# A new hand-written order of work for a two-layer attention kernel, with its loads on one queue

## The chip, the cores and the metric

The kernel runs on one core of a Trainium2 chip. The metric is the time of the whole kernel on the device in microseconds (us), the median of several runs. The profile is of one execution; its span, from the first to the last instruction, is not quite the same number.

## What is computed

Two layers in a row. The first is attention with a local window and a few global keys; the second is a mixture of four attention experts, of which two are taken for each token.

```python
# layer 1: B=4, H=8, S=768, D=64; n_global=8, n_local=96
scores = q @ k.T / sqrt(D) - slope[h] * dist      # dist capped at n_local for global keys
keep   = (key < n_global) | (0 <= row - key < n_local)
x      = softmax(where(keep, scores, -1e9)) @ v   # heads joined: x is [4, 768, 512]
# layer 2: 4 experts of width 64
w      = softmax over the two largest of x @ w_gate
for e in range(4):
    ye   = softmax(causal((x @ wq[e]) @ (x @ wk[e]).T / 8)) @ (x @ wv[e]) @ wo[e]
    out += w[e] * ye                               # for the tokens that chose e
```

## The kernel before

**Tiles.** The work is cut into 24 units of 128 rows: unit u is row block u % 6 of batch u // 6. q, k and v come from memory in float32 and are cast to float16. Layer 1 of a unit: load and cast of q, k, v; transposes of k and q by TensorE (`turn`, L262 to L276) with a copy out of PSUM into kqT; local scores in two halves (`local_scores`, L321: bias by a matmul at L334, k times q at L341, exponential on ScalarE at L344); the few global keys for three units at a time (`global_scores`, L302); the product with v (`local_values`, L360, matmuls at L371) and the division by the row sums into x (L380); a transpose of x (`turn_x`, L383, copy at L390). Layer 2 of a unit: projections to k and q (`project_qk`, L392, matmuls at L401, copy at L406) and to v with the gate (`project_v`, L408, L415, copy at L417); the choice of two experts (`top_two`, L508, in steps); causal scores (L431, matmuls L446, exponential L449), the mask on GpSimd (L461), the product with v (L464, matmuls L474), a transpose (L488) and the output projection (L497, matmul L502, copy L505, store L506).

**Order.** There is no loop over units. The table ORDER, from L760 on, is a list of 658 short names, and a loop at L727 calls one function for each. The schedule is manual: every engine works its own instructions strictly in this order, and waits come from data and buffers. A name has a stage, a number and, where there is a choice, a letter for who does it:

```python
copies = {"a": S_.copy, "g": G.tensor_copy, "v": V.tensor_copy}
queues = {"s": dma, "a": S_.dma_start}
...
for slot in ORDER.split():
    stage, *args = stages[slot[:2]]
    if slot[-1].isalpha():
        args.append(slot[-1])
    stage(int(slot[2:].rstrip("agsv")), *args)
```

The letters on casts and copies are ScalarE (a), GpSimd (g), VectorE (v). On loads, s is the sync engine's queue (SP), which computes nothing, and a is ScalarE's, which must reach the issue in its own order. The names spoken of below: lk, lq load k or q of a unit (0.262 MB, L227). lv loads values (L245, L247): lv0 and lv1 are four pieces of 64 KB each, lv2 to lv5 two of 128 KB, all of batch 0; from lv6 on each is two pieces of 192 KB, and four of them, for four head pairs, make a batch. So a cast of a unit of batch 1 (vc6 to vc11) needs all of lv6 to lv9. wi0 to wi3 load the weights wk, wq, wv (with the gate) and wo (0.524 MB each); wc cast them. kc, qc, vc are casts; tk, tq transposes of k and q; sa, sb local scores; gi, gs, vg, vs the global keys; va, vb attention times v; tx the transpose of x; pk, pq, pv the projections; ro a step of the routing; ca, cb, cc causal scores; ma the mask; za, zb causal times v; tz, ou transpose and output.

**Buffers that make a load or a stage wait.** Four raw buffers each for q and k (a load waits for the cast four units back), two for v by batch, two for weights (wi2 waits for wc0); in PSUM two for scores (psS), one for the products with v (psZ), two for everything else (psT). Stores go on SP's queue too.

Of the kernel before, what the change touches and what calls it, by code (L numbers as in the profile page):

```python
# [757 lines left out]


ORDER = """  # L760
az0 lq0s xb0 lk0s qc0g kc0g tk0 lv0a lk1a vc0g lq1s lk2s kc1g lk3s lq2a lq3s lq4a xg0 tq0a lk4s
tk1 qc1g tq1v wi0a kc2a gi0 kc3v vs0 lv1s sa0 tk2 lq5s qc2g tq2v tk3 lk5a az1 az2 az3 sb0 qc3g
tq3v az4 gs0 vg0 qc4g kc4g lq6s tk4 lv2s wi1a tq4v lk6a sa1 sa2 va0 vb0 sb1 sa3 lv3s kc5v vc1g
lv4s lv5a vg1 va1 vb1 qc5g qc6g sb2 lk7s tk5 tq5v lq7s wc0g wi2a lk8a lk9s tx0v tx1v wc1g kc6v
sa4 sa5 pk0 pk1 lq8s pq0v vc2g vc3v vc4g pq1v vc5g sb3 vg2 gs1 tk6 kc7v lv6s va2 ca0 vb2 lq9a
tq6v sb4 sb5 lk10s lk11a qc7g wc2g tk7 tq7v vg3 va3 tx2v kc8g vb3 kc9v sa6 sb6 lv7s pv0v pv1a
vg4 va4 qc8g qc9g vb4 lv8a lv9s pk2 pq2a tk8 tq8v kc10v lk12s ca1 lk13a vg5 lq10s lq11s va5
tx3v lq12s tk9 tq9v gi1 gs2 tx4v vb5 pv2a pv3a sa7 sa8 tx5v ma0 pk3 ro0 vc6g ro0 vc7v vc8v pq3a
pv4v sb7 ro0 vs1 kc11v pk4 pq4a lq13s tk10 qc10v vc9g kc12v tq10v ca2 cb2 vg6 va6 ro0 vb6 tk11
qc11g ma1 tq11v pv5v ca3 vg7 va7 vb7 cb3 tk12 qc12g tq12v pk5 ro0 qc13g ro0 pq5a ro0 sb8 ro1  # L770
ro1 lv10s gs3 lk14s lk15s tx6v tx7v vg8 va8 vb8 lq14s lq15s lq16s ca4 pv6v pv7v kc13g lk16s
lk17s wi3a qc14v kc14g za0 zb0 sa9 sb9 pk6 pq6a tk13 ro1 tq13v cb4 cc4 ro1 lq17s lq18s qc15g
lv11s vg9 ro1 va9 lv12s tx8v tk14 tq14v vb9 kc15g kc16g lk18s ma2 ma3 ca5 pk7 pq7v tk15 tq15a
sa10 ro1 sb10 za1 pv8v vc10g vc11g qc16g ro1 zb1 pk8 pq8v kc17v tz0a sa11 sa12 vg10 va10 vb10
tz1a lv13s qc17g qc18g ro2 wc3g tk16 tq16v sb11 sb12 tk17 tq17v vg11 ca6 va11 lq19s vb11 gi2
gs4 ou0v ro2 tx9a sa13 sb13 kc18g ma4 vc12g za2 zb2 vc13g vc14g pk9 pq9a vc15g lk19s tx10v vs2
vc16g gs5 tz2v vc17a qc19g pv9v za3 ou1v ca7 cb5 ro2 tx11v lv14s zb3 ro2 pk10 pq10v ou2a vg12
va12 vb12 lk20s lq20s cc5 kc19g lq21a sa14 tk18 tq18v tk19 lk21s tq19v za4 zb4 ro2 ro2 pk11
lv15s pq11a tx12v ca8 vg13 ma5 va13 cb8 ro2 vb13 pv10v pv11a sa15 sa16 ma6 ro3 za5 ma7 tz3v
tx13v ro3 ro3 ro3 zb5 tz4a ro3 sb14 sb15 gi3 pk12 pq12a kc20g pv12v kc21g ca9 cb9 za6 zb6 pk13  # L780
lk22s pq13v kc22g tz5v ma8 ca10 lq22s vg14 va14 vb14 lv16s lv17s ma9 ou3a ou4v sa17 sa18 tz6v
za7 zb7 qc20g tk20 tq20v lk23s tx14v vc18g lq23s cb10 cc10 vg15 va15 vb15 ou5a ou6v sb16 vs3
tx15v ro3 za8 pv13v zb8 pv14a ca11 ca12 pk14 pq14v ro3 za9 vc19g tz7a zb9 sb17 sa19 tz8v ou7v
ma10 gs6 vg16 va16 vb16 qc21g cb11 cc11 ou8v tk21 qc22a tq21v za10 zb10 pk15 pq15a tx16v sb18
sb19 tz9v ro4 tz10v vg17 va17 vb17 ca13 ou9v ou10a vg18 qc23g va18 kc23v vc20g ca14 cb14 ro4
vb18 tk22 pk16 pq16a tq22v ma11 vg19 va19 vb19 ro4 ro4 ro4 ca15 cb15 pv15v pv16v za11 zb11
tx17a sa20 sa21 tx18v ro4 pk17 pq17v pv17a sb20 sb21 vc21g tk23 tq23v tz11a vc22g vg20 va20
vb20 ca16 gs7 ro4 tx19v ro5 pk18 pq18a pk19 ma12 za12 zb12 vc23g pq19a tx20v sa22 sa23 ro5
tz12v ma13 za13 zb13 pv18v ro5 ro5 ma14 ou11a ca17 ro5 vg21 va21 vb21 pk20 pq20v ro5 ro5 pv19a
sb22 sb23 tz13v za14 zb14 tx21v pv20a cb16 cc16 ro6 vg22 ro6 va22 vb22 ou12v ou13a ca18 vg23  # L790
va23 vb23 ro6 ma15 ma16 tx22v pv21a cb17 cc17 ro6 ro6 za15 tz14v zb15 ma17 pk21 pq21v ca19
tx23v za16 tz15v ma18 zb16 pv22a ro6 ro6 pv23a ro7 ca20 cb20 za17 tz16v zb17 ou14a pk22 pq22v
ro7 ro7 ca21 ma19 za18 zb18 ma20 ou15a ou16v ro7 ro7 ca22 cb21 za19 zb19 tz17v pk23 pq23v cb22
ma21 ro7 tz18v za20 zb20 ro7 cc22 ma22 ou17v ca23 tz19v cb23 za21 zb21 ou18v cc23 tz20v za22
zb22 tz21a ou19v ou20a ma23 za23 zb23 tz22a ou21a ou22a tz23v ou23a xt0
"""

MAXB = 512
# [38 lines left out]
```

## Time and profile before

The time is 159.45 us, the median of three runs (159.31 to 162.35). The span of the profiled execution is 160.6 us, TensorE's granted clock 0.946 on average.

| engine | busy us | share of the span | instructions |
|---|---|---|---|
| TensorE, matmul | 134.7 | 84% | 2950 |
| TensorE, weight load | 105.8 | 66% | 2950 |
| VectorE | 112.0 | 70% | 343 |
| ScalarE | 105.4 | 66% | 171 |
| GpSimd | 71.1 | 44% | 187 |

Read from memory are 20.98 MB, written 6.29 MB. SP's queue moved 21.63 MB, ScalarE's 5.65 MB. DMA-issuing instructions aren't counted as busy, so ScalarE's 66% doesn't hold the time in which it issues loads or waits to issue them; the rows named ACTq in a timeline do. Matmuls are pipelined, so a busy TensorE is not one at its peak. In sums by stretch the columns are: length, then busy us (and instructions) of PE, PEld, DVE, ACT and POOL, then the granted clock, the DMA share and GB/s.

### The profile page before, as it was taken

The numbers are of one execution on the slowest core, as the hardware profiler recorded it, in microseconds if no ns is written. First come the engines' busy times: TensorE is split into PE (matmuls) and PEld (weight loads), VectorE is DVE, ScalarE is ACT, GpSimd is POOL, SyncE is SP. The second block draws the span as 40 slices with busy tenths as digits, with TensorE's granted clock in tenths as the row PEclk, the third lists the DMA queues.
The fourth block names the chain that finished last, engine by engine and source line by source line (L and its number), as shares of the span: only waits on it lengthen the run. The fifth ranks groups of instructions, "written<-read, shape, count | busy, mean of one in ns | idle before, by whom it ended". The sixth has DMA issues, their size and how long they took to land.

```text
span 160.6 us, 6996 instructions
## 1 busy us (share of the span) xinstructions
PE 134.7 (84%) x2950; PEld 105.8 (66%) x2950; DVE 112.0 (70%) x343; ACT 105.4 (66%) x171; POOL 71.1 (44%) x187
## 2 busy tenths in 40 slices
PE   0266585779999999899999999999999999999710
PEld 0143363758778879787798876887889778776300
DVE  7978424248769977597796588788866788798530
ACT  0283051074648878788968988989878788799520
POOL 4454343093308463976636643603435254633100
PEclk9999558778999999999999999999999999999995
DMA  5999998999999989795499999032100103042550
GB/s 115 273 288 257 260 236 180 270 257 224 241 256 247 255 189 284 169 225 140 126 227 232 228 293 251 33 131 76 65 6 0 69 6 135 0 172 93 200 208 8
DMA packets 85623, 27.80 MB, mean 173 GB/s; under 512 B 82256, under 2 KB 82256, under 8 KB 85584
## 3 DMA queue, kind: packets, MB, share of 16 engines
q1 hardware_dynamic: 64480, 21.63, 53.6%
q10 hardware_dynamic: 21104, 5.65, 15.8%
q8 instruction: 25, 0.41, 1.1%
q14 instruction: 14, 0.11, 0.2%
HBM read 20.98 MB, written 6.29 MB: 170 GB/s over the span
## 4 chain that ended last, share of the span: by engine, by line
PE 60%; DMA 16%; ACTq 5%; SPq 4%; DVE 3%; ACT 2%; issue 2%; POOL 2%; POOLq 0%
DMA vf<-in_v_dram 11%; PE pps L401 11%; PE vps L415 7%; PE cps L446 6%; PE zps L371 6%; PE tp L267 6%; PE zps L474 5%; PE ops L502 4%; PE sps L334 4%; PE xps L386 4%; SPq L247 3%; DMA kf<-in_k_dram 3%; PE sps L341 3%; ACTq L157 3%; PE zps L356 2%; DMA out_dram<-osb 2%
## 5 line engine op out<-in xcount | busy, mean ns | idle before, releaser
L449 ACT ACTIVATE a<-cps 128x1024 f16<-128x1024 f32 (+1 forms) x48 | 42.0, 915 | 5.7 <-PE cps L446 5.1
L344 ACT ACTIVATE abuf<-sps 128x636 f16<-128x636 f32 (+1 forms) x48 | 30.7, 684 | 20.3 <-PE sps L341 8.5
L259 POOL CAST vbuf<-vf 128x512 f16<-128x512 f32 x20 | 12.3, 637 | 20.5 <-DMA vf<-in_v_dram 9.9
L334 PE MATMUL sps<-biasT,ident 64*64 64x318 f16 (+1 forms) x192 | 16.0, 333 | 5.8 <-ACT abuf L344 5.8
L461 POOL TENSOR_SCALAR_AFFINE_SELECT a<-a 128x256 f16<-128x256 f16 x48 | 18.5, 415 | 5.2 <-ACT a L449 5.2
L276 DVE COPY kqT<-tp 128x1024 f16<-128x1024 f16 x22 | 15.0, 685 | 6.1 <-PE tp L267 5.9
L267 PE MATMUL tp<-ident,s16k 128*128 128x128 f16 x96 | 10.5, 239 | 8.6 <-POOL s16k L255 8.1
L380 DVE TENSOR_TENSOR x<-zps,rinv 128x512 f16<-128x512 f32 x24 | 16.6, 691 | 0.8
L255 POOL CAST s16q<-qf 128x512 f16<-128x512 f32 x21 | 12.9, 622 | 8.6 <-DMA qf<-in_q_dram 5.7
L371 PE MATMUL zps<-vbuf,abuf 64*128 64x65 f16 x704 | 16.7, 195 | 0.0
L341 PE MATMUL sps<-kqT 64*64 64x159 f16 (+2 forms) x384 | 15.6, 243 | 0.8 <-issue 0.7
L371 PEld LDWEIGHTS <-abuf 64*128 64x128 f16 x704 | 15.2, 98 | 1.1 <-issue 0.4
L401 PE MATMUL pps<-xT,wk 128*128 128x128 f16 x192 | 15.4, 227 | 0.0
L474 PE MATMUL zps<-v2buf,a 128*128 128x65 f16 x336 | 15.3, 193 | 0.0
L401 PE MATMUL pps<-xT,wq 128*128 128x128 f16 x192 | 14.9, 223 | 0.0
L474 PEld LDWEIGHTS <-a 128*128 128x128 f16 x336 | 12.9, 97 | 1.7 <-DVE zs L485 0.2
L502 PE MATMUL ops<-wo,zt 128*128 128x512 f16 x48 | 13.5, 380 | 0.4 <-DVE zt L495 0.4
L341 PEld LDWEIGHTS <-kqT 64*64 64x64 f16 x384 | 12.3, 116 | 2.4 <-issue 1.4
L415 PE MATMUL vps<-wvg,xT 128*128 128x260 f16 x96 | 13.7, 274 | 0.0
L267 PEld LDWEIGHTS <-s16k 128*128 128x128 f16 x96 | 6.6, 106 | 10.6 <-POOL s16k L255 8.3
L446 PEld LDWEIGHTS <-kq 64*128 64x128 f16 x336 | 9.7, 94 | 4.9 <-issue 3.8
L446 PE MATMUL cps<-kq,kq 64*128 64x128 f16 x240 | 12.9, 217 | 0.0
(111 smaller groups left out, 267.5 us busy)
## 6 DMA issues: line engine op xcount, KB each, us to landing
out_dram<-osb SPq DMA_DIRECT2D x24, 256.0 KB, 2.3
qf<-in_q_dram SPq DMA_DIRECT2D x20, 256.0 KB, 4.8
kf<-in_k_dram SPq DMA_DIRECT2D x18, 256.0 KB, 4.9
vf<-in_v_dram SPq DMA_DIRECT2D x22, 192.0 KB, 4.4
kf<-in_k_dram ACTq DMA_DIRECT2D x6, 256.0 KB, 5.2
qf<-in_q_dram ACTq DMA_DIRECT2D x4, 256.0 KB, 5.3
vf<-in_v_dram SPq DMA_DIRECT2D x6, 128.0 KB, 6.5
w<-in_moe_wk_dram ACTq DMA_DIRECT2D x1, 512.0 KB, 6.7
```

What stands on the lines that cost most here:

```text
L267: nc.tensor.transpose(tps[u][:, i, p, :], s16s["kq"[i], u][:, 2 * p:2 * p + 2, :].rearrange("j h d -> j (h d)"), ident[:, :])
L334: mm(s_ps[o, hh, 0:2 * w].rearrange("r (c n) -> r c n", c=2), lhsT=ident2[r, :], rhs=biasT[r, p, 0:w].unsqueeze(1).to_broadcast([KB, 2, w] ...
L341: mm(s_ps[o, hh, c * w:c * w + n], lhsT=kqT[b][r, 0, p, k0:k0 + KB], rhs=kqT[b][r, 1, p, k0:k0 + n], start=False, stop=True, skip_group_ch ...
L344: S_.activation(as_[u][:, :, g, :].rearrange("r h (c n) -> r h c n", c=2)[:, :, :, 0:w], s_ps[:, :, 0:2 * w].rearrange("r h (c n) -> r h c ...
L371: mm(zs_[u][:, hf, hq * VW:(hq + 1) * VW], lhsT=as_[u - prev][r, hq % 2, hq // 2, at:at + P], rhs=held("vbuf", u - prev)[r, c, hq, :], sta ...
L401: mm(p_ps[:, i, ep, :], lhsT=w[:, ko, ep, :, :].rearrange("r a d -> r (a d)"), rhs=xT[:, ko, :], start=(i == 0 and ep == 0 and ko == 0), s ...
L415: mm(v_ps[:, :], lhsT=xT[:, ko, :], rhs=wvg16[:, ko, :], start=(ko == 0), stop=(ko == NK - 1))
L446: mm(s_ps[:, e2, i, :], lhsT=kqs[b * NT + ci][r, 0, ep, :], rhs=kqs[u][r, 1, ep, :], start=(i == 0), stop=True, skip_group_check=True)
L449: S_.activation(a2[:, :, 4 * c:4 * c + len(part), :], s_ps[:, :, 0:len(part), :], func=Exp, scale=sc2)
L461: G.affine_select(out=d, in_=d, pattern=[[0, NEP], [1, P]], channel_multiplier=-1, base=0, compare_op=Alu.is_ge, fill=0.0)
L474: mm(z_ps[:, e, :], lhsT=a2[:, e % 2, (e // 2) * n + ci, :], rhs=held("v2buf", b * NT + ci)[:, e, :], start=(e == 0 and ci == 0), stop=Tru ...
L502: mm(o_ps[:, :], lhsT=zts[u][:, ep, :], rhs=wo16[:, ep, :], start=(ep == 0), stop=(ep == NEP - 1))
```

## The change

Only the table is changed: the same 658 stages in another order, with other letters. It is meant to plan with one load queue after the first five loads[...]. What this does:

- All loads go on SP except lk1 and lv0, which stay on ScalarE. Before, six lk, four lq, three lv and all four wi were on ScalarE.
- The loads come in another order: all of batch 0 (q, k, v) and wi0, wi1, wi2 before anything of batch 1. Before, q and k of units 6 and 7 came ahead of wi2, and q and k of units up to 12 ahead of the last values of batch 1.
- wi3 moves from far ahead of its cast wc3 to directly ahead of it.
- Letters change on casts and copies:

| stage | before | after |
|---|---|---|
| kc | g 13, v 10, a 1 | g 14, v 7, a 3 |
| qc | g 21, v 2, a 1 | g 17, v 5, a 2 |
| vc | g 20, v 3, a 1 | g 16, v 7, a 1 |
| wc | g 4 | g 3, a 1 (wc2) |
| tq | v 22, a 2 | v 19, a 5 |
| tx | v 22, a 2 | v 17, a 7 |
| pq | v 12, a 12 | v 13, a 11 |
| pv | v 13, a 11 | v 12, a 12 |
| tz | v 17, a 7 | v 19, a 5 |
| ou | v 12, a 12 | v 10, a 14 |

The table's first part, which the lead-in follows, and its end:

```diff
-az0 lq0s xb0 lk0s qc0g kc0g tk0 lv0a lk1a vc0g lq1s lk2s kc1g lk3s lq2a lq3s lq4a xg0 tq0a lk4s
-tk1 qc1g tq1v wi0a kc2a gi0 kc3v vs0 lv1s sa0 tk2 lq5s qc2g tq2v tk3 lk5a az1 az2 az3 sb0 qc3g
-tq3v az4 gs0 vg0 qc4g kc4g lq6s tk4 lv2s wi1a tq4v lk6a sa1 sa2 va0 vb0 sb1 sa3 lv3s kc5v vc1g
-lv4s lv5a vg1 va1 vb1 qc5g qc6g sb2 lk7s tk5 tq5v lq7s wc0g wi2a lk8a lk9s tx0v tx1v wc1g kc6v
-sa4 sa5 pk0 pk1 lq8s pq0v vc2g vc3v vc4g pq1v vc5g sb3 vg2 gs1 tk6 kc7v lv6s va2 ca0 vb2 lq9a
-tq6v sb4 sb5 lk10s lk11a qc7g wc2g tk7 tq7v vg3 va3 tx2v kc8g vb3 kc9v sa6 sb6 lv7s pv0v pv1a
-vg4 va4 qc8g qc9g vb4 lv8a lv9s pk2 pq2a tk8 tq8v kc10v lk12s ca1 lk13a vg5 lq10s lq11s va5
-tx3v lq12s tk9 tq9v gi1 gs2 tx4v vb5 pv2a pv3a sa7 sa8 tx5v ma0 pk3 ro0 vc6g ro0 vc7v vc8v pq3a
+az0 lk0s lq0s lq1s xb0 lk1a kc0a lk2s lk3s tk0 kc1v lv0a qc0v qc1v tk1 tq0a lq2s tq1a lk4s xg0
+lk5s lv1s kc2a kc3g kc4v tk2 tk3 qc2a tq2a vc0g vs0 az1 az2 az3 gi0 sa0 lq3s sb0 qc3g lq4s az4
+wi0s lq5s sa1 gs0 tk4 wi1s lv2s lv3s tq3a sa2 kc5g tk5 vc1g qc4g qc5g tq4a sb1 vg0 wc0g va0 vb0
+sa3 tq5v sb2 tx0a wc1g vg1 lv4s va1 vb1 sa4 lv5s sb3 sb4 vg2 vc2v vc3v sa5 pk0 vc4g sb5 tx1a
+wi2s pq0a gs1 va2 vb2 pk1 pq1v wc2a tx2v vg3 vc5g va3 vb3 ca0 pk2 pq2v pv0a lq6s qc6g ca1 lq7s
+lk6s lk7s kc6g lk8s vg4 lv6s va4 vb4 lq8s lv7s pv1a pv2a ro0 kc7a qc7g kc8v tk6 tq6v ca2 cb2
+tk7 tq7v lv8s lv9s vg5 va5 vb5 gi1 tx3a tx4v ro0 sa6 sb6 tk8 qc8g tq8v pk3 pq3v ro0 ro0 gs2 pk4
+pq4v tx5v lk9s sa7 vc6v vc7g sb7 lq9s pv3v lq10s pv4v vs1 ca3 pv5v pk5 vc8g ro0 vc9v vg6 va6
...
+tx11a sa14 vc12g vs2 qc17g zb3 pk9 lq18s qc18g tk17 lk18s tq17v wi3s kc18v pq9a ro2 ro2 wc3g
...
+va15 cb10 vb15 pk13 pq13v ou5a sa18 sa19 ro3 tx14v lk23s tk21 tq21v vg16 va16 vb16 gs6 ro3
+tx15a ma8 pv13v ca11 cb11 tz6v ro3 ro3 za8 zb8 pk14 pq14v ma9 vc17g pv14a cc10 cc11 ro4 za9
+tz7v zb9 ro4 pk15 tz8a lv17s vc18g vc19v ma10 pq15v sb18 sb19 vg17 kc22g va17 vb17 ou6a tx16v
...
-zb22 tz21a ou19v ou20a ma23 za23 zb23 tz22a ou21a ou22a tz23v ou23a xt0
+ou19a ou20v za23 zb23 ou21a tz22v tz23v ou22a ou23v xt0
```

More of the change, by code (lines that the diff above doesn't have):

```diff
@@ L767 @@
-vg4 va4 qc8g qc9g vb4 lv8a lv9s pk2 pq2a tk8 tq8v kc10v lk12s ca1 lk13a vg5 lq10s lq11s va5
-tx3v lq12s tk9 tq9v gi1 gs2 tx4v vb5 pv2a pv3a sa7 sa8 tx5v ma0 pk3 ro0 vc6g ro0 vc7v vc8v pq3a
[L769 to L794, printed above, removed]
-zb22 tz21a ou19v ou20a ma23 za23 zb23 tz22a ou21a ou22a tz23v ou23a xt0
+az0 lk0s lq0s lq1s xb0 lk1a kc0a lk2s lk3s tk0 kc1v lv0a qc0v qc1v tk1 tq0a lq2s tq1a lk4s xg0
@@ new lines @@
+pq4v tx5v lk9s sa7 vc6v vc7g sb7 lq9s pv3v lq10s pv4v vs1 ca3 pv5v pk5 vc8g ro0 vc9v vg6 va6
+cb3 vb6 pq5a kc9g qc9g tk9 tq9v ca4 ro0 lk10s lk11s lq11s qc10g lq12s vg7 kc10g va7 vb7 tx6a
+kc11g tk10 tq10v sa8 sb8 pv6v qc11g lk12s vc10v lq13s tk11 tq11v vg8 cb4 va8 vb8 ma0 cc4 qc12v
+ma1 pk6 pq6a ma2 tx7v sa9 sb9 tx8v ro0 za0 zb0 pv7v gs3 lk13s vc11a kc12g tk12 tq12v kc13g ro1
+lv10s lk14s sa10 sb10 vg9 va9 vb9 qc13g tz0a ro1 tk13 ro1 kc14g lq14s lk15s tq13v sa11 sb11
+lk16s za1 zb1 pk7 pq7a tx9v sa12 sb12 tk14 qc14g tq14v tz1v vg10 ro1 ma3 kc15g lq15s qc15g
@@ new lines @@
+lq16s lq17s ca5 va10 vb10 ro1 ma4 lv11s kc16g lv12s ro1 ro1 pv8a pv9a cb5 cc5 za2 zb2 pk8 tx10v
+pq8a ca6 gi2 vg11 va11 qc16a vb11 sa13 tz2v tk15 tq15v gs4 lv13s ro2 lk17s tk16 tq16v kc17v za3
+tx11a sa14 vc12g vs2 qc17g zb3 pk9 lq18s qc18g tk17 lk18s tq17v wi3s kc18v pq9a ro2 ro2 wc3g
+lk19s ca7 lk20s vg12 va12 vb12 gs5 lq19s lq20s tk18 tq18v vc13g lq21s pv10a za4 vc14g zb4 tx12a
+kc19v sb13 ma5 ma6 lk21s sb14 ou0v vc15g vc16g ou1a vg13 va13 vb13 qc19g ca8 ca9 pv11v pk10 ro2
+ro2 pq10v ou2a qc20v za5 cb8 kc20v cb9 tz3v tx13v zb5 pk11 ro2 ro2 ro3 pq11a tk19 tq19v qc21g
@@ new lines @@
+sa15 sb15 za6 zb6 tk20 tq20v ro3 pv12a ro3 sa16 sa17 lv14s lv15s vg14 va14 vb14 tz4a ma7 lq22s
+lq23s pk12 pq12v kc21g sb16 sb17 qc22g tz5v za7 gi3 lv16s zb7 ou3a lk22s qc23v ou4v ca10 vg15
+va15 cb10 vb15 pk13 pq13v ou5a sa18 sa19 ro3 tx14v lk23s tk21 tq21v vg16 va16 vb16 gs6 ro3
+tx15a ma8 pv13v ca11 cb11 tz6v ro3 ro3 za8 zb8 pk14 pq14v ma9 vc17g pv14a cc10 cc11 ro4 za9
+tz7v zb9 ro4 pk15 tz8a lv17s vc18g vc19v ma10 pq15v sb18 sb19 vg17 kc22g va17 vb17 ou6a tx16v
+sa20 vs3 ro4 tx17v tz9v za10 zb10 ou7a tk22 tq22v ca12 ca13 vg18 va18 vb18 vc20g vc21g vc22v
@@ new lines @@
+kc23g ro4 pv15a pv16v sa21 vg19 va19 vb19 ro4 ro4 ca14 ma11 pk16 pq16a tx18v sb20 sb21 tx19v
+ro4 pv17v ro5 ro5 za11 tk23 tq23v zb11 pk17 pq17v tz10v gs7 ca15 ro5 vg20 va20 ma12 vb20 ou8a
+pv18v ro5 sa22 sb22 ro5 ma13 tz11v za12 zb12 vc23g pk18 ou9a ro5 pq18v ca16 vg21 va21 vb21 cb14
+pv19v tx20v cb15 vg22 va22 ma14 vb22 ma15 ca17 pk19 tx21v pq19a za13 zb13 cb16 cb17 tz12v ou10v
+za14 pk20 pq20a tz13v zb14 sa23 sb23 pv20v ro5 ro6 pv21a za15 zb15 ro6 ro6 ro6 ro6 ou11a ou12v
+cc16 cc17 vg23 va23 ro6 vb23 pk21 pq21a ou13v ca18 ca19 ma16 ma17 ma18 tx22v za16 tx23v zb16
@@ L796 @@
+pv22a pv23a ma19 ca20 ca21 tz14v za17 ro6 ro7 tz15v tz16v ro7 zb17 ou14a pk22 pq22v cb20 cb21
+tz17v za18 zb18 ro7 ro7 ou15a ou16v ca22 cb22 za19 zb19 ro7 pk23 ma20 pq23v za20 zb20 tz18a
+cc22 ca23 ro7 tz19v ma21 ou17v cb23 ro7 za21 zb21 ou18v cc23 tz20v ma22 ma23 za22 zb22 tz21a
+ou19a ou20v za23 zb23 ou21a tz22v tz23v ou22a ou23v xt0
 """
```

## The prediction

> **What bounds the kernel now.** I read the slices of the span first, then sums by stretch, then ScalarE's timeline where TensorE stands still, then the waits. Two stages with different limits appear.
>
> The slices (40 of 4.0 us; tenths busy, granted clock, DMA share, GB/s):
>
> ```profile
> PE   0266585779999999899999999999999999999710
> ACT  0283051074648878788968988989878788799520
> PEclk9999558778999999999999999999999999999995
> DMA  5999998999999989795499999032100103042550
> GB/s 115 273 288 257 260 236 180 270 257 224 241 256 247 255 189 284 169 225 140 126 227 232 228 293 251 33 131 76 65 6 0 69 6 135 0 172 93 200 208 8
> ```
>
> TensorE is full from slice 10 (40 us) to slice 37. Before that it is half used, at a clock down to 0.5, while DMA is full. The sums by stretch say the same:
>
> ```profile
> 0.00:16.00 16.00, 6.33 (x76) 4.16 (x77) 12.97 (x49) 5.52 (x8) 7.58 (x21) 1.00 1.07 233
> 16.00:40.00 24.00, 17.63 (x352) 14.14 (x351) 10.53 (x22) 7.96 (x13) 10.24 (x23) 0.72 1.11 238
> 40.00:145.00 105.00, 103.43 (x2423) 83.53 (x2423) 82.17 (x249) 85.65 (x141) 51.76 (x140) 1.00 0.61 156
> ```
>
> 428 of 2950 matmuls are started in the first 40 us; the other 105 us take 2423. ScalarE in the stretch 15 to 40 us:
>
> ```profile
> 18.43 1.36 ACTq L227 DMA_DIRECT2D kf<-in_k_dram  x1
> 19.84 1.29 ACT L344 ACTIVATE abuf<-sps 128x636 f16<-128x636 f32 x2 [4.15 <-DVE s16k L255]
> ...
> 24.98 1.56 ACTq L247 DMA_DIRECT2D vf<-in_v_dram  x2
> 26.59 0.70 ACT L344 ACTIVATE abuf<-sps 128x636 f16<-128x636 f32 x1 [3.91 <-PE sps L341]
> 26.67 0.55 ACTq L149 DMA_DIRECT2D w<-in_moe_wv_dram  x1
> 27.26 4.31 ACTq L157 DMA_DIRECT2D wg<-in_moe_w_gate_dram  x1
> 31.66 0.47 ACTq L227 DMA_DIRECT2D kf<-in_k_dram  x1
> 32.18 1.97 ACT L344 ACTIVATE abuf<-sps 128x636 f16<-128x636 f32 x3 [4.88 <-issue]
> ```
>
> The exponentials (L344) stand behind loads that ScalarE has to issue: it idles 4.15, 3.91 (in part for TensorE, which had its own delay) and 4.88 us, and TensorE loses 5.8 us to it in the first 40 us:
>
> ```profile
> POOL vbuf L259 <- DMA vf<-in_v_dram: 9.9, 3, 5.9
> PE sps L334 <- ACT abuf L344: 5.8, 3, 2.5
> ACT abuf L344 <- issue: 4.9, 1, 4.9
> ```
>
> The first of these lines is the other limit: value loads. The last one of batch 1 (lv8, lv9: both halves of each) lands at 47.70 us in the trace, and the cast behind it, vc6, starts at 47.85 after GpSimd has idled 6.15 us.
>
> [...] with both queues loaded (4 to 14 us) 282 GB/s, with SP's alone (49 to 57 us) 245. [...] 0.72 was granted from 16 to 40 us, 1.00 from 40 on.
>
> **A yardstick.** From 45 to 145 us I take the mean spacing from one matmul's start to the next (gaps over 250 ns left out) by kind: pps 57 ns x384, zps of attention 17 x704, vps 124 x96, tp 62 x192, causal cps 34 x336, its zps 32 x336, ops 218 x48, and so on; all together 122 us of full-clock TensorE work. By this measure the kernel has done 15 us at 40 us, and has 100.6 left when vc6 starts; from there to the end of the span are 160.55 - 47.85 = 112.7 us. So behind 40 us nearly nothing can be gained, and ahead of it up to 25 us are lost. A gain must come from reaching the same point of the work earlier.
>
> **The change, part by part.**
>
> (1) Loads off ScalarE. Before, 23 issues there take 17.7 us, 9.8 of them between 8 and 40 us; after, lk1 and the four pieces of lv0 stay, some 3.2 us by the same rows (0.6 to 0.7 each), all before 9 us. The waits above (up to 12.9 us of ScalarE, 5.8 of TensorE) go. SP gets these issues; it computes nothing, so what stands behind a blocked issue is only later loads and, from ou0 on, stores.
>
> (2) Work put onto ScalarE, by the counts in the table: kqT copies 2 to 5 (1.01 each), xT copies 2 to 7 (0.585), casts of k and q 2 to 5 (0.62), the wv cast (4 of 0.37, as the copy L417 of that size takes, and the gate's 0.2), osb 12 to 14 (0.585), less three small ones: about +9.7 us. The lead-in takes most: five kqT copies, three casts, two xT copies, twelve exponentials of 0.684, wv and others, 22.7 us from about 5 us on; so ScalarE can be through by 28 to 30, and is not the limit unless it waits. VectorE loses 3 us, GpSimd 6: nothing, both have idle time.
>
> (3) A shared queue's rate. The trace of before doesn't show SP alone in the lead-in. Bounds: 221 GB/s (the stretch 20 to 30 us) and 282; I take 245, the stretch in which it was alone.
>
> (4) Loads reordered: batch 0 and the first three weight sets ahead of batch 1. Before, 10.75 MB had landed when lv9 came at 47.70 (23 loads of 0.262 MB, v of two batches 3.15, weights 1.57); after, lv9 stands behind 18 of them only, 9.44 MB. First bytes move at 2.4 us and a load lands some 1.3 us after its bytes (both from before's first 16 loads), so lv9 lands at 9.44/0.245 + 3.7 = 42.2 us. Buffers don't delay it: each q or k load waits for the cast four units back, and the casts of units 0 to 5 need loads that land by 20. wi2 waits for the cast of wi0, which ends near 22, when SP gets to it.
> The wait for wi2: 6.30 MB, 25.7 + 3.7 = 29.4 us, against 34.4 (gate 35.8) before; its cast moves to ScalarE, so pv0 can start near 31, against 39.57. At pv0 14.1 us of TensorE work are done; up to vc6 8.9 more follow, so TensorE gets to the wait for lv9 at about 40 to 41 and waits some 1.5 us there. That wait takes the place of ScalarE's.
>
> Sum: vc6 starts at 42.4 instead of 47.85, with 100.2 instead of 100.6 left: 5.5 + 0.4 = 5.9 us earlier. What follows is TensorE's, at the same 0.89 us of work per us of span up to the end (tail included); the last stores are as before. The wo load (wi3) directly ahead of its cast in the list, and lv17 behind ou5, cost nothing if SP runs ahead, as it does by four units. 159.45 - 5.9 = 153.5 us.
>
> **Rivals.**
> (B) A single queue supplies less. At 221 GB/s lv9 lands at 46.4: gain 1.3 + 0.4, 157.7 us. For: the rate dips to 180 in slice 6, where small v pieces stand in a row, and after has eight in a row. Against: 247 to 256 GB/s in slices 11 to 13, largely SP alone.
> (C) The v load isn't the limit. At 282 GB/s it lands at 37.2 and pv0 binds, which ScalarE's 22.7 us hold at about 30.5: 9.1 us earlier with 0.8 us more work left, so 151.2. [...] Against: no stretch of one queue had 282.
> (D) New waits behind 40 us. ScalarE is at 85.65 of 105 us there; if all of its added 9.7 us came onto the path, 153.5 + 9.7 = 163.2, slower. For: a cast that waits for a load (kc7 on ScalarE, vc6 on VectorE) now stands ahead of PSUM copies, and TensorE with two psT buffers stops behind them. Against: removed issues outweigh the added work (14.4 to 9.7), and at 82% it has room.
>
> **How the numbers follow.** Forecast 0.54, B 0.18, C 0.17, D 0.11. Predicted is 153.5. The range 150 to 159 takes in B and C with an error of 1 us, and leaves out D. Faster by over 2% is below 156.3: most of forecast and C, a little of B: 0.70. Within 2%: 0.20. Slower: 0.10, from D.
>
> **What would show it.** Right: no ScalarE idle over 2 us put down to issue or a late load between 10 and 30 us; the last batch-1 v load landing at 42 +- 1; pv0 (first L415) near 31; the TensorE row full from about 32 us but for a dip of 1 to 2 us near 41, and as dense behind it as before. Wrong: a rate under 230 GB/s between 10 and 40 us (B), full TensorE straight from 31 (C), or gaps of TensorE behind ScalarE or VectorE after 45 us (D). If v lands by 42 and the time isn't below 157, the step that says the rest goes at the same pace is wrong.

## The result, and the profile after

The changed kernel takes 167.35 us (median of five runs, 166.42 to 168.99) against 159.45 of the kernel before: the ratio is 1.049, with an interval from 1.039 to 1.058. It is slower, where 153.5 was forecast. Here and below a time is the median of all runs, while a ratio with its interval is taken from the fast runs alone, because some executions of a kernel are slower than the rest; so it isn't quite the quotient of two medians.

The page's slices of the changed kernel (40 slices of 4.2 us; the rows are the busy tenths of TensorE and ScalarE, the granted clock, the share of the DMA engines, and what they moved):

```profile
PE   0547698698988599894999997999999999999500
ACT  3459478578377498974588784988858988898300
PEclk9999999999999999998799999999999999999965
DMA  5997977999789789988998896703003015133530
GB/s 123 266 252 174 246 169 169 220 251 243 180 186 247 173 192 238 223 191 183 265 221 261 186 232 212 166 4 126 6 4 131 4 63 194 52 140 126 192 137 10
```

TensorE is fed earlier (6 to 9 tenths from slice 3 on, and the clock is full in place of the dip to 5 before), but it isn't full from 40 us on: there are holes at slices 13 (54 us), 18 (75 to 79 us) and 24. The DMA row has sevens and eights where it had nines. The same stretches as before (length; busy us and instructions of PE, PEld, DVE, ACT, POOL; clock; DMA share; GB/s):

```profile
0.00:16.00 16.00, 6.82 (x81) 4.43 (x81) 10.90 (x49) 8.43 (x12) 3.37 (x14) 1.00 0.89 200
16.00:40.00 24.00, 19.96 (x446) 14.82 (x439) 10.46 (x24) 16.78 (x31) 9.65 (x20) 1.00 0.97 214
40.00:145.00 105.00, 96.97 (x2249) 79.16 (x2250) 74.94 (x225) 79.28 (x131) 49.11 (x129) 0.98 0.64 159
```

In the first 40 us 527 matmuls start instead of 428, although the transfers are slower (200 and 214 GB/s instead of 233 and 238). Then 2249 follow in the 105 us in which there were 2423. By the yardstick of the prediction (full-clock TensorE work done, in us):

| at | 40 us | 50 | 60 | 65 | 75 | 80 | 90 | 110 | 150 |
|---|---|---|---|---|---|---|---|---|---|
| before | 15.0 | 24.1 | 33.4 | 38.4 | 47.3 | 52.1 | 62.1 | 81.9 | 120.4 |
| after | 18.6 | 26.8 | 33.9 | 38.5 | 47.8 | 49.4 | 58.5 | 76.8 | 116.2 |

So the change is 3.6 us of work ahead at 40 us, level at 65, and 5.1 behind at 110. It loses in three steps: 45 to 60 us, 75 to 85 us, and about 100 us. From 4.2 us of work behind at 150 us to the 6.5 us by which the two spans differ at the end some 2 us more are lost in the tail; no experiment below takes the tail apart.

ScalarE between 18 and 29 us, as its timeline has it (start and length in us, instruction, and in brackets the idle time before it):

```profile
19.84 0.70 ACT L344 ACTIVATE abuf<-sps 128x636 f16<-128x636 f32 x1 [0.58 <-PE sps L341]
20.80 1.01 ACT L276 COPY kqT<-tp 128x1024 f16<-128x1024 f16 x1 [0.26 <-PE tp L267]
...
25.48 2.47 ACT L344 ACTIVATE abuf<-sps 128x636 f16<-128x636 f32 x4 [0.26 <-PE sps L341]
28.23 0.60 ACT L344 ACTIVATE abuf<-sps 128x512 f16<-128x512 f32 x1 [0.28 <-PE sps L341]
```

The waits of 4.15, 3.91 and 4.88 us ahead of the exponentials are gone; what is left is half a us at a time, for TensorE. The waits of the changed kernel (engine and line, what it waited for, us in total, times, longest):

```profile
POOL s16q L255 <- DMA qf<-in_q_dram: 16.9, 8, 4.8
...
POOL vbuf L259 <- DMA vf<-in_v_dram: 10.5, 3, 5.3
POOL s16k L255 <- DMA kf<-in_k_dram: 10.1, 5, 7.8
```

All three are casts on GpSimd that wait for loads, of q and k as much as of v. Around the second loss the timeline shows how one of them reaches TensorE:

```profile
75.00 0.31 PE L341 MATMUL sps<-kqT 64*64 64x159 f16 x8
...
77.03 0.61 POOL L259 CAST vbuf<-vf 128x512 f16<-128x512 f32 x1 [5.31 <-DMA vf<-in_v_dram]
77.58 0.61 POOL L255 CAST s16q<-qf 128x512 f16<-128x512 f32 x1
77.69 0.32 PE L295 MATMUL vgps<-vbuf,sel 64*64 64x65 f16 x8 [2.38 <-POOL vbuf L259]
```

The values of batch 2 (the last of them lv13) land at 76.9; GpSimd, which has stood 5.31 us, casts them, and TensorE starts again 2.4 us late. In the kernel before this load had landed at 74.2.

The loss at 100 us begins at a load too. VectorE stands 2.25 us for q of unit 23, whose cast has the letter v in the new table and had g in the old; the copy of an output (L505) is next on VectorE, and TensorE stands for that copy:

```profile
100.06 0.47 DVE L255 CAST s16q<-qf 128x512 f16<-128x512 f32 x1 [2.25 <-DMA qf<-in_q_dram]
100.45 0.68 DVE L505 COPY osb<-ops 128x512 f32<-128x512 f32 x1
...
101.18 0.59 PE L502 MATMUL ops<-wo,zt 128*128 128x512 f16 x2 [1.23 <-DVE osb L505]
```

Where the transfers fell behind is in the sums from 4 to 75 us, first of the kernel before, then of the changed one (last column GB/s):

```profile
4.00:75.00 71.00, 57.50 (x1236) 45.96 (x1237) 47.94 (x135) 39.84 (x66) 35.75 (x79) 0.90 1.06 236
```

```profile
4.00:75.00 71.00, 57.41 (x1249) 44.14 (x1253) 41.92 (x129) 49.36 (x83) 28.43 (x64) 1.00 0.95 213
```

236 GB/s for 71 us are 16.8 MB, 213 are 15.1. So by 75 us the changed kernel is 1.6 MB behind (23 GB/s for 71 us). Of this 0.52 MB is wi3, which the new table puts off on purpose (issued at 77.7 us, before at 58.4); the other 1.1 MB are some 5 us at its rate. The chain that ended last says it too: SP's issues have 21% of it (4% before) and transfers 22% (16%).

```profile
PE 38%; DMA 22%; SPq 21%; DVE 6%; POOL 4%; issue 4%; ACT 1%; DVEq 0%; POOLq 0%; ACTq 0%
```

SP is issuing, or held in an issue (an issue is "held" when it takes far longer than the row's usual time), for 29.5 of the 31 us from 14 to 45, and 27.7 of the 30 us up to 75 (17.6 and 22.1 before). How an issue holds it, and what follows, from SP's timeline and from the sums by stretch:

```profile
17.65 0.87 SPq L149 DMA_DIRECT2D w<-in_moe_wq_dram  x1
18.56 3.56 SPq L247 DMA_DIRECT2D vf<-in_v_dram  x1
```

```profile
17.50:18.50 1.00, 0.90 (x8) 0.52 (x9) 0.00 (x0) 0.25 (x1) 1.00 (x3) 1.00 1.25 284
...
22.00:22.50 0.50, 0.50 (x16) 0.32 (x14) 0.21 (x2) 0.42 (x1) 0.09 (x1) 1.00 0.20 44
22.50:23.50 1.00, 0.80 (x16) 0.43 (x8) 0.69 (x1) 0.56 (x1) 1.00 (x3) 1.00 0.63 145
```

One piece of v (128 KB) is issued at 18.56 and the issue isn't done before 22.12. By then the queue has run dry: 44 GB/s, and then 145; the pieces that follow are 128 KB each and take 0.635 us of issue, which allows 206 GB/s at most. Yet the same single queue moved 284 GB/s at 18 us. It is not a slow queue but one with holes. Of the 122 half microseconds from 14 to 75 us, 23 moved less than 150 GB/s in the changed kernel and 41 more than 250; in the kernel before it was 12 and 55.

### The profile page after: what moved, and what is told of

It reads as the page before. It is cut to its first block, busy times and chain, and to the rows that moved or that the text cites. A ratio compares the mean times of both kernels' runs of the same rounds, so it can differ in the third digit from the quotient of the medians.

```text
span 167.1 us, 6994 instructions
## 1 busy us (share of the span) xinstructions
PE 135.6 (81%) x2950; PEld 105.7 (63%) x2950; DVE 108.2 (65%) x339; ACT 114.4 (68%) x187; POOL 65.9 (39%) x175
## 2 busy tenths in 40 slices
DMA packets 85624, 27.81 MB, mean 166 GB/s; under 512 B 82256, under 2 KB 82256, under 8 KB 85584
## 4 chain that ended last, share of the span: by engine, by line
PE 38%; DMA 22%; SPq 21%; DVE 6%; POOL 4%; issue 4%; ACT 1%; DVEq 0%; POOLq 0%; ACTq 0%
DMA qf<-in_q_dram 13%; SPq L247 12%; PE pps L401 7%; SPq L227 5%; PE cps L446 5%; PE zps L474 5%; PE ops L502 5%; DMA vf<-in_v_dram 5%; PE vps L415 4%; PE zps L371 3%; DMA kf<-in_k_dram 2%; DMA out_dram<-osb 2%; PE xps L386 2%; SPq L245 2%; POOL a L461 2%
## 5 line engine op out<-in xcount | busy, mean ns | idle before, releaser
L344 ACT ACTIVATE abuf<-sps 128x636 f16<-128x636 f32 (+1 forms) x48 | 30.9, 685 | 6.9 <-PE sps L341 6.3
L255 POOL CAST s16q<-qf 128x512 f16<-128x512 f32 x17 | 10.4, 612 | 22.1 <-DMA qf<-in_q_dram 16.9
L276 DVE COPY kqT<-tp 128x1024 f16<-128x1024 f16 x19 | 13.0, 687 | 6.0 <-PE tp L267 5.7
L371 PE MATMUL zps<-vbuf,abuf 64*128 64x65 f16 x704 | 15.2, 190 | 1.6 <-DVE vbuf L259 1.6
L259 POOL CAST vbuf<-vf 128x512 f16<-128x512 f32 x16 | 10.3, 660 | 14.7 <-DMA vf<-in_v_dram 10.5
L401 PE MATMUL pps<-xT,wk 128*128 128x128 f16 x192 | 15.1, 223 | 0.5 <-DVE lg L421 0.5
L371 PEld LDWEIGHTS <-abuf 64*128 64x128 f16 x704 | 14.2, 94 | 2.1 <-issue 1.7
L341 PE MATMUL sps<-kqT 64*64 64x159 f16 (+2 forms) x384 | 15.0, 237 | 0.7 <-ACT kqT L276 0.7
L401 PE MATMUL pps<-xT,wq 128*128 128x128 f16 x192 | 15.1, 223 | 0.0
L267 PE MATMUL tp<-ident,s16q 128*128 128x128 f16 x96 | 10.8, 244 | 4.6 <-POOL s16q L255 3.8
L378 DVE RECIPROCAL rinv<-zps 128x8 f32<-128x8 f32 x24 | 4.9, 205 | 12.9 <-PE zps L371 12.3
```

Source lines behind the costliest of these rows:

```text
L267: nc.tensor.transpose(tps[u][:, i, p, :], s16s["kq"[i], u][:, 2 * p:2 * p + 2, :].rearrange("j h d -> j (h d)"), ident[:, :])
L344: S_.activation(as_[u][:, :, g, :].rearrange("r h (c n) -> r h c n", c=2)[:, :, :, 0:w], s_ps[:, :, 0:2 * w].rearrange("r h (c n) -> r h c ...
L371: mm(zs_[u][:, hf, hq * VW:(hq + 1) * VW], lhsT=as_[u - prev][r, hq % 2, hq // 2, at:at + P], rhs=held("vbuf", u - prev)[r, c, hq, :], sta ...
L401: mm(p_ps[:, i, ep, :], lhsT=w[:, ko, ep, :, :].rearrange("r a d -> r (a d)"), rhs=xT[:, ko, :], start=(i == 0 and ep == 0 and ko == 0), s ...
```

## The experiments

Two theories to begin with. **Q**: one queue supplies less, and this is what costs (rival B of the prediction, grown). **P**: the new order and the new letters cost, as stores, casts and loads stand in the way of each other behind 40 us (rival D). The ratios are to the kernel before on the same chip, whose medians there were 160 to 162 us; the runs were spread over several chips, so kernels are best compared by ratio.

**Queue or table.** e1 takes the table of before and gives it the changed kernel's queue letters:

```diff
-tk1 qc1g tq1v wi0a kc2a gi0 kc3v vs0 lv1s sa0 tk2 lq5s qc2g tq2v tk3 lk5a az1 az2 az3 sb0 qc3g
+tk1 qc1g tq1v wi0s kc2a gi0 kc3v vs0 lv1s sa0 tk2 lq5s qc2g tq2v tk3 lk5s az1 az2 az3 sb0 qc3g
 (and so for every load but lk1 and lv0)
```

> The table of before, with every load moved to SP's queue except lk1 and lv0; nothing else is changed. Theory Q (one queue of 256-byte pieces delivers some 210 GB/s, SP being busy issuing from the start to about 100 us, so all loads come late): 165 to 170 us. Rival P (the queue is fine, the new order and letters are what costs): ScalarE is relieved and nothing else moves, 155 to 160 us.

Measured: 166.24 us, ratio 1.026 (1.009 to 1.043). The queue alone costs some 4 us (by the interval 1.4 to 7): Q. That is about half of the changed kernel's loss, whose ratio is 1.049 (1.039 to 1.058). The values of batch 1 land at 52.0 instead of 47.7, and 14 to 45 us moves 207 GB/s, SP issuing for 29.2 of those 31 us.

e2 is the reverse: the changed table with the queue letters of before (17 loads on ScalarE).

```diff
-wi0s lq5s sa1 gs0 tk4 wi1s lv2s lv3s tq3a sa2 kc5g tk5 vc1g qc4g qc5g tq4a sb1 vg0 wc0g va0 vb0
+wi0a lq5s sa1 gs0 tk4 wi1a lv2s lv3s tq3a sa2 kc5g tk5 vc1g qc4g qc5g tq4a sb1 vg0 wc0g va0 vb0
 (and so for lk5, lk6, lk8, lk11, lk13, lq2, lq4, lq9, lq21, lv5, lv8, wi2, wi3)
```

> The table of after, with each load on the queue on which before had it (17 of them on ScalarE). Theory Q: loads arrive at 235 to 250 GB/s again, the wait near 75 us goes; 157 to 162 us, some of it lost to ScalarE's blocked issues. Rival P: 166 to 170 us, since order and letters are those of after.

Measured: 179.82, ratio 1.122 (1.109 to 1.135), which neither theory had. SP's queue waits, in this run:

```profile
SPq L247 <- DMA wg<-in_moe_w_gate_dram: 5.6, 1, 5.6
SPq L247 <- DMA qf<-in_q_dram: 5.6, 2, 4.2
SPq L247 <- DMA kf<-in_k_dram: 5.5, 2, 4.9
```

SP's issues wait here for loads that ScalarE issues, and issues late, because in the changed table it reaches them late (the gate's at 34.4 us, where it is held for 2.3; at 27.3 in the kernel before); SP issues for only 8.8 of the 31 us from 14 to 45. In this run the second queue is no help, as its engine comes late to its issues: 184 GB/s in that stretch. The letters and the order belong together, and this pair isn't a fair trial of two queues.

**Is the order good, if loads come?** e3 (changed table) and e4 (table of before) read the same bytes in long contiguous runs.

```diff
-        queues[on](f[:, :, :], {"k": k, "q": q}[nm][b, :, ri * P:(ri + 1) * P, :]
-                   .rearrange("h j d -> j h d"))
+        queues[on](f[:, :, :], {"k": k, "q": q}[nm][b, :, :, :].rearrange("h s d -> (h s) d")
+                   [ri * P * H:(ri + 1) * P * H, :].rearrange("(j h) d -> j h d", h=H))
...
-                           .rearrange("(c j) d -> j c d", j=KB))
+                           .rearrange("(j c) d -> j c d", j=KB))
```

> The table of after as it is; the loads of q, k and of v from batch 0's second part on read the same bytes in contiguous runs (2 KB for q and k, 2 to 3 KB for v) instead of 256-byte pieces, so rows land at other places and the output isn't the attention of the inputs; all stages run as before. Theory Q: SP's queue is no longer full, TensorE runs dense from about 30 us; 150 to 155 us. Rival P: the plan itself costs, 163 to 168 us.

> The table of before with the same contiguous loads as in the run of after's table (the same part of the computation changed). Theory Q: 153 to 158 us, and not faster than after's table with these loads, since only ScalarE's blocked issues remain. Rival P: also 153 to 158 us, but then after's table is slower than this by 5 us or more.

Measured: e3 157.17, ratio 0.979 (0.961 to 0.997); e4 162.52, ratio 1.005 (0.999 to 1.010). e3 lies 2 us above Q's range and 6 below P's, e4 some 4.5 us above both. The new order is faster than the old by 5 us once loads come fast enough, and about 7% of the time of before faster than with its own loads: P falls, in the form that the new order costs by itself. With the short supply of one queue the new order isn't better than the old: 1.049 here against 1.026 in e1, on two chips and with intervals that just overlap. The old order gains nothing from faster loads, though its stretch 14 to 45 us moved 267 GB/s. In e3 TensorE stands nowhere for over half a us between 25 and 142 us:

```profile
4.00:75.00 71.00, 64.15 (x1442) 50.90 (x1443) 47.56 (x146) 55.50 (x96) 36.45 (x80) 1.00 0.86 252
```

252 GB/s is what this order took in e3; with its own loads it got 213.

**Which part of the loads.** g1 makes only q and k long (the first half of the diff above), g2 only v (the second), g5 leaves the runs and gives more buffers:

```diff
-    raw = fast.enter_context(tc.tile_pool(name="raw", bufs=4))
+    raw = fast.enter_context(tc.tile_pool(name="raw", bufs=7))
```

> After's table; q and k loads read the same number of bytes in runs of 2 KB instead of 256 B (so it isn't the attention of these inputs: the rows reach the wrong heads and units); v is as in after. With q, k and v long it was 157.2. Theory R (the number of 256-byte descriptors of q and k, 1024 a load, is what blocks SP's issues): most of that gain comes back, 158 to 161 us, the values of batch 1 landing by 43. Theory I (the fixed price of v's small pieces is what starves the queue): 164 to 167, batch 1's values landing at 45 to 46.5.

> After's table; each v piece of lv2 and on reads the same number of bytes in runs of 2 or 3 KB a partition (its rows come in another order, so it isn't the attention of these inputs); q and k are as in after. The number of v pieces is unchanged. Theory R: 164 to 167, since v has half as many descriptors as q and k. Theory I, if what a v piece costs is its descriptors: 158 to 161; if it is the issue itself, whatever its descriptors: 165 to 168.

> After with seven raw buffers each for q and k instead of four; nothing else changes. Theory B (SP's long issues are waits for a buffer, that is for the cast four units back): they go, the stretch 14 to 45 us moves 225 GB/s or more, 158 to 163 us. Theory R or I (they are the queue's own limit): 165 to 168, the same rate of 208 to 212.

Measured: g1 157.64, ratio 0.981 (0.975 to 0.986); g2 162.31, ratio 1.018 (1.004 to 1.032); g5 166.67, ratio 1.042 (1.030 to 1.053). By descriptors the contiguous runs are meant of which a load consists. Long runs in q and k bring nearly all of the gain; long runs in v bring a little under half of it; buffers bring nothing clear of the noise. g1 is somewhat faster than Theory R had it, though the values of batch 1 landed only at 44.3; g2 falls between the ranges. The two gains add up to more than both together (6.8% and 3.1% of the time of before against 7.0%), as they would if either brings the supply near to what the order takes. g1 by stretch, then its loads of q and k (line, instruction, and ns of one issue, shortest/median/longest), and the same line of the changed kernel:

```profile
14.00:45.00 31.00, 26.73 (x570) 19.85 (x561) 14.55 (x33) 21.30 (x38) 11.11 (x24) 1.00 0.97 218
45.00:75.00 30.00, 29.55 (x732) 24.63 (x733) 22.68 (x67) 25.85 (x44) 22.55 (x52) 1.00 0.92 281
```

```profile
L227 SPq DMA_DIRECT2D qf<-in_q_dram x24: 327/422/2090, 1.3 to 85.3; - x24
```

```profile
L227 SPq DMA_DIRECT2D qf<-in_q_dram x24: 453/954/2837, 1.3 to 94.4; - x24
```

An issue of q takes 0.42 us instead of 0.95. Behind 45 us, where q and k make up most of what is loaded, the rate goes from 208 to 281 GB/s; ahead of it only from 210 to 218; there the eight pieces of batch 0's v and the weights stand, which g1 leaves as they are. Long runs change two things at once, the time that SP spends in an issue and the number of pieces that the transfer itself consists of (42616 packets in g1's whole execution, 85624 in the changed kernel's); these runs don't tell the two apart. A piece of v takes 0.65 us of issue with 256-byte runs and 0.595 with long ones. Counted over the first 100 us, SP's loads were held longer than 1.25 us:

| kernel | such issues | us in them | us in all load issues |
|---|---|---|---|
| after | 21 | 40.9 | 88.6 |
| g5, seven buffers | 22 | 41.0 | 87.1 |
| g2, long v | 19 | 37.9 | 85.8 |
| g1, long q and k | 10 | 22.7 | 66.0 |
| e3, all long | 8 | 14.4 | 53.8 |

**One late load, or the whole supply.** The span of these kernels follows the moment at which batch 2's values are cast (77.0 us in after, 72.6 in g2, 66.4 in g1, 63.7 in e3). h1 and h2 therefore move these loads alone:

```diff
-ma1 pk6 pq6a ma2 tx7v sa9 sb9 tx8v ro0 za0 zb0 pv7v gs3 lk13s vc11a kc12g tk12 tq12v kc13g ro1
-lv10s lk14s sa10 sb10 vg9 va9 vb9 qc13g tz0a ro1 tk13 ro1 kc14g lq14s lk15s tq13v sa11 sb11
+ma1 pk6 pq6a ma2 tx7v sa9 sb9 tx8v ro0 za0 zb0 pv7v gs3 lk13s vc11a kc12g tk12 tq12v kc13g ro1
+lv10s lv11s lv12s lv13s lk14s sa10 sb10 vg9 va9 vb9 qc13g tz0a ro1 tk13 ro1 kc14g lq14s lk15s tq13v sa11 sb11
 (h1; in h2 lv11s lv12s lv13s stand ahead of lk16s)
```

> After with lv11, lv12 and lv13 directly behind lv10, so that seven loads of q and k (1.84 MB) stand behind the values of batch 2 instead of ahead of them. Theory V (the one load lv13, awaited from 75 to 77.7 us, sets the end): the cast of these values starts near 70 instead of 77, 159 to 163 us. Theory S (the queue's whole supply sets it, and whatever is put ahead delays what is put behind): the wait moves to the casts of q and k of units 14 to 17, 165 to 169.

> After with lv11, lv12 and lv13 ahead of lk16, that is four loads of q and k (1.05 MB, 5 us at 210 GB/s) earlier. Theory V: the cast of batch 2's values starts near 72, 161 to 164 us. Theory S: 165 to 168.

Measured: h1 166.71, ratio 1.041 (1.021 to 1.061); h2 170.13, ratio 1.061 (1.038 to 1.083). Theory S, and h2 even somewhat beyond it. In h1 the values of batch 2 landed at 65.9 us instead of 76.9, and nothing was gained. The wait moved: TensorE now stands for k of a later unit,

```profile
67.56 0.61 PE L267 MATMUL tp<-ident,s16k 128*128 128x128 f16 x4 [3.22 <-POOL s16k L255]
```

and at 80 us h1 has done 49.1 us of work, after 49.4. In h2 a cast of q on GpSimd waited 7.40 us for its load, and TensorE stood 6.97 us, from 68 to 75, for what came behind that cast. These values' load alone doesn't set the end; what is put behind it comes late in its turn.

**Two repairs.** f1 puts wi0 to wi3 of the changed table on ScalarE (four letters); f2 puts wi2 with the gate of the table of before on SP (one letter), where ScalarE had lost 4.88 us to it.

```diff
-sa3 tq5v sb2 tx0a wc1g vg1 lv4s va1 vb1 sa4 lv5s sb3 sb4 vg2 vc2v vc3v sa5 pk0 vc4g sb5 tx1a
-wi2s pq0a gs1 va2 vb2 pk1 pq1v wc2a tx2v vg3 vc5g va3 vb3 ca0 pk2 pq2v pv0a lq6s qc6g ca1 lq7s
+sa3 tq5v sb2 tx0a wc1g vg1 lv4s va1 vb1 sa4 lv5s sb3 sb4 vg2 vc2v vc3v sa5 pk0 vc4g sb5 tx1a
+wi2a pq0a gs1 va2 vb2 pk1 pq1v wc2a tx2v vg3 vc5g va3 vb3 ca0 pk2 pq2v pv0a lq6s qc6g ca1 lq7s
 (f1; likewise wi0, wi1, wi3. In f2: wi2a becomes wi2s in the table of before)
```

> The table of after with only wi0 to wi3 (and the gate) moved to ScalarE's queue, 5 issues, at the same places. Theory Q: 1.57 MB of the first 9.44 MB come beside SP's loads, so the last v of batch 1 lands some 4 to 6 us earlier; later loads gain less; 160 to 165 us. Rival P (order and letters): 166 to 169 us.

> The table of before with wi2 (wv and the gate) moved from ScalarE's queue to SP's. If ScalarE's block of 4.3 us behind the gate's load costs what the trace of before says (TensorE 1.9 us idle behind it): 156 to 159 us beside the 159 to 161 of before. If SP's queue pays it back by delaying the loads behind: 159 to 162 us.

Measured: f1 169.17 with 162.38 of before beside it (no ratio can be given), no gain, where Theory Q had 160 to 165 and P 166 to 169; f2 163.84, ratio 1.005 (0.999 to 1.011), no gain either. In f1 the stretch 14 to 45 us moved 216 GB/s, but 45 to 75 only 191, and pv0 started at 37.1 instead of 34.5: ScalarE comes to issue wi2 only at 29.2 us and is then held for 2.97 us in the issue of the gate. In f2 pv0 started at 36.2 instead of 39.6, but batch 1's values were cast at 49.3 instead of 47.9: paid back. f2 shows something else too: its SP is issuing for 28.9 of the 31 us from 14 to 45, with 21 issues held over 1.25 us in the first 100, as in the changed kernel, and yet it moves 228 GB/s from 4 to 75 us and is as fast as before (its profiled execution took 166.2 us). A full SP row is thus not enough to make a kernel slow.

**The rate by itself.** The loads of q and k alone, 48 of them into buffers of their own with a sum and a store behind, leaving out all else: s1 on one queue, s2 on two in turn. Then all loads of a table without the computing, each into a buffer of its own: t1 after's on one queue, t2 after's on two, t3 before's on one, t4 before's on two. The edit of s1 and s2 is shown; t1 to t4 run the table with only the names lk, lq, lv and wi left in it.

```diff
+    qs = (dma,)                # s2: (dma, S_.dma_start)
+    for n in range(48):
+        u, src = n // 2, (k, q)[n % 2]
+        b, ri = divmod(u, NT)
+        f = raw.tile([P, H, Dh], F32, name=f"f{n}")
+        qs[n % len(qs)](f[:, :, :], src[b, :, ri * P:(ri + 1) * P, :].rearrange("h j d -> j h d"))
```

> Only the 48 loads of q and k (0.262 MB each, the same 256-byte pieces), each into a buffer of its own, all on SP's queue, then sums of pairs and the stores; attention and experts are left out. Theory Q: 205 to 220 GB/s over the loads, with an issue of 1.3 us or more again and again. Rival R (the queue alone carries 245 GB/s, what slowed it in the changed kernel were its buffer waits): 240 to 260 GB/s.

> The same loads, every other one on ScalarE's queue (the same parts are left out). Theory Q: 270 to 288 GB/s. Rival R: no more than 10% above the run with one queue.

> Only the loads of the table of after, in its order, on its queues (SP, with lk1 and lv0 on ScalarE), each into a buffer of its own so that no cast is waited for, then 24 stores; all computing is left out. Theory Q (one queue is the limit): 205 to 220 GB/s. Theory M (the memory limits pieces of 256 bytes by which loads are in flight together, whatever the queue, as the two streams with 218 GB/s each suggest): 205 to 220. Theory W (buffer and lane waits limit): 245 or more.

> The same loads in the same order with the queue letters of before (17 names on ScalarE's queue); computing left out. Theory Q: 250 to 285 GB/s. Theory M: within 5% of the run with one queue.

> The loads in the order of the table of before, all on SP but lk1 and lv0; computing left out. Theory Q: 205 to 220 GB/s. Theory M: the order decides, so as fast as before's own queues, 235 or more.

> The loads in the order of the table of before on its own queues; computing left out. Theory Q: 250 to 285 GB/s. Theory M: as before's order on one queue, 235 or more. If all four are 215 to 220, neither queue nor order sets the rate, and what differs in the kernels is how well the queues are kept filled.

Measured, one execution each: s1 79.37 us, s2 79.31; t1 to t4 121.8, 121.8, 122.7, 122.5. The stretch 14 to 45 us of s1, then of s2, and 4 to 75 us of t4 (here only the engines that ran have a column; the last three are clock, DMA share and GB/s):

```profile
14.00:45.00 31.00, 9.00 (x13) 0.00 (x0) 1.00 1.35 218
```

```profile
14.00:45.00 31.00, 9.00 (x13) 0.00 (x0) 1.00 1.35 218
```

```profile
4.00:75.00 71.00, 0.00 (x0) 1.00 1.35 213
```

Second queue or not, this order or that: 207 to 213 GB/s in all four tables' loads, 218 for q and k. The part of Q that a second queue raises what these loads can reach by themselves (270 to 288 was expected for s2, 250 to 285 for t2 and t4) is wrong, and so is Theory M, which had 235 or more for the old order. In the kernels the second queue did raise it: from 4 to 14 us before moved 282 GB/s, e1, the same table on one queue, 247. These loads also ran differently from those in the kernels: a DMA share of 1.35 for 213 GB/s, against 1.06 for 236 in the kernel before. A packet thus took longer (about 25 ns by the trace's packet records, against 18 in the kernels). So in these streams, which never stop, the 256-byte packets themselves were slower; in the changed kernel they were fast, and the queue has holes (under 150 GB/s in 23 of the 122 half microseconds from 14 to 75 us, in t1 in 3). The two end near the same mean, 213, and why the packets slow down in the stream isn't settled.

**All kernels in one table**, by what they moved from 4 to 75 us in the profiled execution:

| kernel | GB/s, 4 to 75 us | time as a ratio to before |
|---|---|---|
| e2 | 193 | 1.122 |
| f1 | 208 | 1.042 (quotient of the medians) |
| after | 213 | 1.049 |
| h2 | 216 | 1.061 |
| g5 | 218 | 1.042 |
| e1 | 218 | 1.026 |
| h1 | 223 | 1.041 |
| f2 | 228 | 1.005 |
| g2 | 228 | 1.018 |
| e4 | 234 | 1.005 |
| before | 236 | 1 |
| g1 | 252 | 0.981 |
| e3 | 252 | 0.979 |

A slow kernel also asks for less, so the table by itself shows no cause; but g1 and g2 changed nothing in the computing but the order of the rows, and e1 nothing but the queue, and they lie in the same order.

## Why the prediction was wrong

**Step 1, loads off ScalarE: right.** The three waits are gone, ScalarE's idle time ahead of the exponentials (L344) fell from 20.3 to 6.9 us, and at 40 us the kernel is 3.6 us of work ahead. The losses behind 40 us begin at loads (54, 75 and 100 us). Rival D's premise, that a cast which waits for a load stands ahead of PSUM copies and stops TensorE, came true at 100 us on VectorE, for 1.2 us; behind ScalarE it isn't seen in the three losses.

**Step 2, ScalarE's added work hidden: right.** ScalarE is busy 114.4 us instead of 105.4, and e3 has the same added work and no wait for it to speak of.

**Step 3, a single queue's rate: mis-sized, and the first cause.** 245 GB/s was taken, from the one stretch of before in which SP was alone; measured were 210 (14 to 45 us) and 213 (4 to 75). In the terms of the sum, 9.44 MB from 2.4 to 45.3 us (lv9's landing at 46.6 less 1.3), it was 220, the lower bound of 221 that the prediction had named. The stretch of 245 was eight us long and held six loads of q and k and two v pieces of 192 KB; it was a short sample of a rate that swings. What was missed is the issuing: 85 load issues, 21 of them held for 1.3 to 3.6 us, make 88.6 of the first 100 us of SP, and the queue has holes. e1 shows that the one queue costs some 4 us by itself, g1 that with long runs in q and k this order on one queue is faster than the kernel before. That the issues are what binds is argued and not shown: SP's row is full in f2 too, which is as fast as before, and from 49 to 57 us in before, where it moved the 245.

In the streams two issuers together reached what one did (s1 218 GB/s, s2 218). In the kernel the second issuer was worth something all the same: SP's load issues fill 88.6 of the first 100 us of the changed kernel, and e1 lost 2.6% by giving the second issuer up.

**Step 4, lv9 at 42.2, the wait for wi2 at 29.4, pv0 near 31: wrong by step 3.** lv9 landed at 46.6, wi2 at 32.3, pv0 began at 34.5. The bytes were counted rightly: 200 GB/s up to 16 us are 3.20 MB, 214 from there to 40 us are 5.14, and the other 1.10 of the 9.44 MB take up to 45.3 us at 208; with 1.3 us to land that is the measured 46.6. It is rival B's number (46.4) nearly to the letter. In e3 the same table gave a cast of these values at 42.2 and pv0 at 31.6, which are the forecast's numbers, and behind that cast it went on at 0.89 us of work per us, to a span of 153.5. So the sum held where the loads came.

**Step 4's last part, "What follows is TensorE's, at the same 0.89 us of work per us": wrong, and the larger error.** Rival B kept this and so gave 157.7. At the cast of batch 1's values (46.8 us) 24.2 us of work were done, 97.8 left; at 0.89 the span would have been 46.8 + 109.9 = 156.7. It was 167.1, at 0.81 of work per us. The forecast, as a span, was 160.6 - 5.9 = 154.7; of the 12.4 us that were missing, 2.0 came from the lead-in and 10.4 from behind it. The prediction ended its accounting of transfers at lv9. But the queue goes on at 208 GB/s up to 75 us where before had 219, and the deficit, most of it made ahead of 45 us, falls due at q of unit 11 (54.5 to 56.5 us), at the values of batch 2 (75.1 to 77.7) and at q of unit 23 (TensorE stands until 101.2 for a copy behind its cast). The line by which one could have known was before's from 45 to 75 us (below it the changed kernel's):

```profile
45.00:75.00 30.00, 29.15 (x713) 23.91 (x711) 23.77 (x65) 23.70 (x41) 18.07 (x43) 1.00 0.95 219
```

```profile
45.00:75.00 30.00, 26.49 (x652) 21.55 (x655) 20.84 (x60) 22.92 (x38) 16.08 (x38) 1.00 0.92 208
```

TensorE was full there with a DMA share of 0.95, and the values of batch 2 were cast at 74.31, 0.1 us after they had landed: the transfers had little slack to give away. How much of the 10.4 us is the supply and how much the order that meets it isn't separated; e1 with the old order lost less on one queue.

The chance of slower was put on rival D alone. The way it came, B with its deficit carried to the end, was not among the rivals.

## What to carry to other kernels

When loads are gathered on one queue, add up the issuing engine's time: number of loads times the issue row's duration, and the issues that are held, against the time until the data are due; if it comes near the whole stretch, look for holes in the queue, and test it: of the 31 us from 14 to 45 SP was issuing for 29.5 in the changed kernel, 29.2 in e1 and 28.9 in f2; the first two lost 4.9% and 2.6%, f2's ratio was 1.005. A rate that a queue showed for a few us needn't be the one that it keeps up through a table: here it was 245 GB/s for 8 us in the kernel before, and 213 for 71 us in the changed one. And a shortfall of bytes isn't over at the first load that is late: follow the bytes to the end of the loading, and ask how much slack the old kernel's transfers had there.

## What the runs showed of the hardware that was not expected

- Loads of 256-byte runs reached much the same rate from 14 to 45 us on one queue (s1 218 GB/s, t1 and t3 206) and on two (s2 218, t2 207, t4 211), with nothing else running but s1's and s2's sums, and packets took about 25 ns then; within the changed kernel one queue reached 284 GB/s for a us, with packets of about 18 ns. Why isn't settled.
- An issue of a v piece on 64 partitions took 0.61 to 0.65 us whether it moved 64, 128 or 192 KB, and 0.595 with long runs; an issue of 256 KB on 128 partitions could be done in 0.37 to 0.45 us, and in 0.33 with long runs. Pieces of 128 KB issued one after another in 0.635 us each come to 206 GB/s at most, an estimate from these numbers.
- Issues on SP's queue were held for 1.3 to 3.6 us again and again; it happened less often with fewer descriptors (21 times in 100 us, 10 with long q and k), and as often with more buffers (22 with seven). What holds them within the queue isn't shown by any view.
- With the changed table on two queues (e2) loads of the one queue waited for loads of the other: SP stood 5.6 us for the gate's load, which ScalarE issued at 34.4 us.
